# Adding the weights' lower words in one VectorE instruction, with the plan's due times set anew

## The chip, the cores and the metric

One core of a Trainium2 chip runs the program. The metric is the device time of one execution in microseconds (us), lower is better. A profiled execution gives the trace; the runs without a profile give the time.

## The reference

Random-feature attention (8 batches of 8 heads, 576 tokens, head size 64, 128 features) is followed by a two-layer network with an ELU on 4608 tokens; both weight matrices come as float64.

```python
q_s, k_s = (q * scale, k * scale)                 # q, k, v: (8, 8, 576, 64)
def phi(x):
    proj = np.einsum('bhsd,md->bhsm', x, omega)   # omega: (128, 64)
    sq = np.sum(x * x, axis=-1, keepdims=True) / 2.0
    h = proj - sq
    h = h - np.max(h, axis=-1, keepdims=True)
    return np.exp(h) / np.sqrt(m)
q_p, k_p = (phi(q_s), phi(k_s))
kv = np.einsum('bhsm,bhsd->bhmd', k_p, v)
z = np.sum(k_p, axis=2)
num = np.einsum('bhsm,bhmd->bhsd', q_p, kv)
den = np.einsum('bhsm,bhm->bhs', q_p, z)[..., None] + 1e-06
x = (num / den) laid out as (4608, 512)
h = x @ w_in                                      # (512, 2048)
g = np.where(h > 0.0, h, np.exp(np.minimum(h, 0.0)) - 1.0)
out = g @ w_out                                   # (2048, 512)
```

## The kernel before

**The work.** Two heads make a pair, and 32 pairs make the attention, four to a batch. Of a pair, keys and queries are projected (TensorE into `ppk` and `ppq`), their exponentials taken on ScalarE (`hk`, `hq`, line 463), the key-value product made (`pkv`), the queries divided by their sums on VectorE and GpSimd, turned over and multiplied by the key-value product (`pn`); ScalarE and VectorE write the result to `xh` (a rounded high part) and `xl` (the rest, line 851). The network runs in 192 steps, numbered F: a step takes 128 of the 2048 hidden units for a block of 384 tokens. Layer 1 is 12 matmuls into `ph` (lines 970 to 972, three for each of four chunks, because weights and activations are each split in a high and a low part). `ph` has two buffers, and a buffer is free once VectorE's line 983 has read it. The ELU takes two ScalarE instructions (979, 980) and that VectorE one into `e`; `e` is split into the two halves of `g` (the low half by `TENSOR_TENSOR` at the helper line 386, on GpSimd or VectorE). Layer 2 is 9 matmuls (1008 to 1010) of `g` with `w2h` and `w2l` into `acc`. Steps 0 to 23 use half the hidden units for each of blocks 0 to 2, steps 24 to 47 the other half; from step 48 on a block takes 16 steps.

**The conversion.** The weights arrive as 64-bit numbers, and `from_f64` makes 32-bit ones of them, 32 tiles of 128x512 in all (16 of the first layer, 16 of the second), most of them while blocks 0 to 2 run their first half. `raw` holds the two words of each number side by side; `u` is the tile that becomes the weight. A conversion is, in order: a load into `raw`; a scaled copy of the upper words into `u` on ScalarE (line 898); a scaled copy of the lower words in place on ScalarE (902), which leaves their top three bits as a small integer; a clamp (906), a shift (910) and the sign (915) on VectorE; the add of the lower words' bits to `u` on GpSimd (918); the high half by a copy on ScalarE or VectorE (381 or 383) and the low half by a subtraction (386) into `w1c`, or `w2h` and `w2l`.

**What sets the order.** The kernel records every piece of work as a task with an engine, a cost in ns, a due time in us and what it reads and writes. A planner (`Plan.order`) then goes through time: whenever an engine is free, it gives it the ready task with the earliest due time, by its costs and by its latencies between engines. What comes out is a fixed order for each engine; the instructions are issued in it and wait for each other by semaphores. Some tasks name a second engine and go to where the planner has them end sooner. A task with `port=True` is kept apart in time from GpSimd's tasks when it runs on VectorE. While the planned time is under `YIELD` (220 us), GpSimd's first instruction of a task is also made to wait for the VectorE task that the plan started last before it:

```python
                if eng == "POOL" or eng == "DVE" and port:
                    held[eng] = now + ns
                    if now < YIELD:
                        self.behind[best] = last.get("DVE") if eng == "POOL" else None
                    last[eng] = best
```

The due times come from the constants at the top (`MLP0`, `SEG`, `STEP`, `STEP_ATT` for the steps; `DUE_*`, `LOAD2`, `K2`, `KV2`, `Q2` for a pair's parts ahead of its end; `CONV*` for the conversions).

Of the kernel before, what the change touches and what calls it, by code (L numbers as in the profile page):

```python
# [42 lines left out]

MLP0 = 45.16
SEG = [8.6, 5.97, 3.67, 5.16, 3.34, 5.69]
STEP = 5.29
STEP_ATT = 6.32

LAG = 3.35


PAIR0 = 8.61
DUE_LOAD, DUE_K, DUE_KV, DUE_Q = 24.84, 25.17, 14.25, 18.96
LOAD2, K2, KV2, Q2 = 72.76, 36.27, 29.03, 29.75
TAIL = 12.89
TAIL2 = 5.01


CONV1 = 11.46
CONV_STEP = 0.11  # L60
CONV2 = 0.74

EARLY = 23.11
CONV3 = 52.47

# [3 lines left out]

DUE_Z = 13.38  # L70


TURNED = 8
EARLIER = 11.0
QB = 32
# [220 lines left out]

YIELD = 220e3
ENGINES = dict(DVE=mybir.EngineType.DVE, POOL=mybir.EngineType.Pool)
# [5 lines left out]
def other(kind, *engs):  # L304
    return () if ALT[kind] is None else [(eng, ns, ALT[kind]) for eng, ns in zip(engs[::2], engs[1::2])]


def mm(n, m=1):

    return m * (n / 2.23 + 2.5)  # L310


def act(n, psum=False, ptr=False):
    return (51 if psum else 93) + 0.833 * n + (93 if ptr else 0)

# [10 lines left out]
def performer_elu_kernel(  # L326
# [125 lines left out]
    def project(i, nm, due):  # L452
# [15 lines left out]
        if native(i, nm):  # L468
            for a in range(2):
                def square(e, a=a):  # L470
                    if e == "ACT":
                        nc.scalar.activation(x()[D:P, a], x()[0:D, a], AF.Square)
                    else:
                        tt(e, x()[D:P, a], x()[0:D, a], x()[0:D, a], ALU.mult)

                op(
                    "ACT", act(S), due - 3 + a, square, ((x, a),), ((x, a, 2),),
                    alt=other("sq", "POOL", pool(S), "DVE", dve(S)), port=True,
                )
            for g in range(3):  # L480
# [16 lines left out]

                op("PE", 872 if g < 2 else 240, d, mms, [*((x, a, 2) for a in range(2)), "of"], (p,))
                op(
# [20 lines left out]
        for a in range(2):  # L520
# [3 lines left out]
            op(  # L524
                "ACT", 694, due - 5 + a, lambda e, r=r, cs=cs: copy(e, y()[r, cs], x()[r, 0]), parts, ((y, a, "h"),),
                alt=other("y_hi", "DVE", dve(S, True)), port=True,
# [6 lines left out]
        for c in range(5):  # L533
# [13 lines left out]

            op("PE", mm(256, n), d, mms, [(y, a, z) for a in range(2) for z in "hl"] + ["oh", "om"], (p,))
            def rest(c=c, n=n, p2=p2, view=view):
# [145 lines left out]
    def finish(i, due):  # L695
# [25 lines left out]
        for g in range(3):  # L721
# [18 lines left out]

            op("DVE", len(slots) * 209, d, dens, (hg, pz), ((den, g),))
            op("DVE", 100, d + 0.5, lambda dg=dg: nc.vector.reciprocal(dg(), dg()), ((den, g),), ((den, g),))  # L742
# [58 lines left out]
    def output(i, halves, more=None):  # L801
# [8 lines left out]
        def mms():  # L810
# [57 lines left out]
    def from_f64(src, hi, lo, nm, due, key):  # L868
# [13 lines left out]
        def low():  # L882
            return words()[:, :, 0]
# [4 lines left out]
        def ui():  # L888
            return u().bitcast(I32)


        op(
# [267 lines left out]
```

## Time and profile before

| | |
|---|---|
| median of 3 runs | 1020.78 us (1020.41 to 1021.74) |
| the profiled execution | 1021.72 us, of which the trace's span is 1019.9 us |
| TensorE (PE) busy | 1005.0 us, 99% |
| ScalarE (ACT) busy | 698.5 us, 68% |
| VectorE (DVE) busy | 646.0 us, 63% |
| GpSimd (POOL) busy | 404.3 us, 40% |
| granted clock of TensorE | 1.0 of full speed throughout |

The span runs from the first instruction of the program to the end of the last; 1.8 us of the profiled execution lie around it. A busy share is an average over the whole span: the four engines are loaded very differently in its first 185 us, where the weights are converted, and after it.

### The profile page before, as it was taken

What the parts mean: (1) busy time and instruction counts of PE and PEld (TensorE: products, weight loads), DVE (VectorE), ACT (ScalarE), POOL (GpSimd) and SP (SyncE); (2) the same over time, 40 slices, a digit from 0 to 9 for tenths busy, and PEclk for the clock granted to TensorE, in tenths of its full rate; (3) what the DMA queues carried; (4) which work ended last, traced back from release to release, by engine and by line L of the source; (5) the groups of instructions that cost most, each with busy time, mean ns of one, the idle gap of its engine ahead of it and who ended that gap; (6) DMA issues with size and microseconds to landing.
All of it is one profiled execution on the core that took longest, in us unless ns stands there. A gap on an engine that the chain in (4) does not pass through costs nothing.

```text
span 1019.9 us, 19153 instructions
## 1 busy us (share of the span) xinstructions
PE 1005.0 (99%) x5923; PEld 890.8 (87%) x5923; DVE 646.0 (63%) x2451; ACT 698.5 (68%) x1887; POOL 404.3 (40%) x421
## 2 busy tenths in 40 slices
PE   8999999999999999999999999999999999999998
PEld 7778788998888888998888988999888888899997
DVE  6999878768978872246877874227777775222221
ACT  7989775669978983268888995338889886322222
POOL 2544444414644452233454543224445454222221
PEclk9999999999999999999999999999999999999999
DMA  8656686667697765436766867434667754533431
GB/s 212 210 194 211 217 292 229 248 201 255 224 307 237 251 212 183 158 131 219 239 209 215 246 217 243 156 124 174 229 217 229 251 155 163 186 130 132 162 128 52
DMA packets 70518, 205.24 MB, mean 201 GB/s; under 512 B 7952, under 2 KB 20432, under 8 KB 70416
## 3 DMA queue, kind: packets, MB, share of 16 engines
q1 hardware_dynamic: 70416, 204.01, 60.7%
q8 instruction: 48, 0.79, 0.3%
q14 instruction: 54, 0.44, 0.1%
HBM read 169.64 MB, written 34.34 MB: 200 GB/s over the span
## 4 chain that ended last, share of the span: by engine, by line
PE 88%; DVE 5%; ACT 4%; issue 1%; POOL 1%; DMA 1%; SPq 0%; POOLq 0%; DVEq 0%; ACTq 0%
PE ph L970 13%; PE acc L1008 12%; PE acc L1009 12%; PE ph L972 12%; PE ph L971 12%; PE acc L1010 12%; PE ppq L543 3%; PE ppk L543 3%; PE pn L820 2%; PE pkv L649 1%; PE pn L649 1%; ACT hk L463 1%; PE pkv L602 1%; PE ppq L493 1%; PE ppk L493 1%
## 5 line engine op out<-in xcount | busy, mean ns | idle before, releaser
L386 POOL TENSOR_TENSOR g<-e,g 128x384 fp32r<-128x384 f32 x173 | 183.8, 1064 | 386.9 <-DVE g L383 326.0
L970 PE MATMUL ph<-xh,w1c 128*128 128x384 f32 x768 | 263.1, 343 | 3.4 <-DVE e L983 2.7
L972 PE MATMUL ph<-xh,w1c 128*128 128x384 f32 x768 | 258.9, 337 | 0.0
L971 PE MATMUL ph<-xl,w1c 128*128 128x384 f32 x768 | 258.0, 336 | 0.0
L983 DVE SCALAR_TENSOR_TENSOR e<-e,ph 128x384 f32<-128x384 f32 x192 | 105.7, 552 | 216.7 <-ACT e L980 214.9
L979 ACT ACTIVATE e<-ph 128x384 f32<-128x384 f32 x192 | 94.8, 494 | 200.6 <-PE ph L972 193.6
L1008 PE MATMUL acc<-w2h,g 128*128 128x512 f32 x576 | 228.3, 396 | 0.0
L1009 PE MATMUL acc<-w2l,g 128*128 128x512 f32 x576 | 226.8, 394 | 0.0
L1010 PE MATMUL acc<-w2h,g 128*128 128x512 f32 x576 | 225.3, 391 | 0.0
L970 PEld LDWEIGHTS ph<-xh,w1c 128*128 128x128 f32 x768 | 144.2, 188 | 19.4 <-DVE e L983 4.8
L971 PEld LDWEIGHTS ph<-xl,w1c 128*128 128x128 f32 x768 | 144.4, 188 | 9.3
L972 PEld LDWEIGHTS ph<-xh,w1c 128*128 128x128 f32 x768 | 144.0, 187 | 0.3 <-DVE w1c L386 0.3
L1010 PEld LDWEIGHTS acc<-w2h,g 128*128 128x128 f32 x576 | 108.1, 188 | 24.6 <-POOL g L386 0.3
L1008 PEld LDWEIGHTS acc<-w2h,g 128*128 128x128 f32 x576 | 108.2, 188 | 11.4 <-issue 1.2
L1009 PEld LDWEIGHTS acc<-w2l,g 128*128 128x128 f32 x576 | 108.3, 188 | 7.9
L386 POOL TENSOR_TENSOR hq<-hq,den 128x512 f32<-128x512 f32 (+1 forms) x96 | 79.4, 839 | 76.9 <-DVE den L742 39.7
L980 ACT ACTIVATE e<-e 128x384 f32<-128x384 f32 x192 | 100.8, 527 | 3.2
L552 ACT ACTIVATE p2k<-ppk,sqk 128x128 f32<-128x128 f32 x225 | 69.7, 366 | 22.0 <-PE ppk L543 21.4
L733 DVE CUSTOM_DVE_ANT_0 junk<-hq,pz 128x128 f32<-128x128 f32 (+1 forms) x320 | 74.0, 280 | 4.6 <-PE pz L712 3.5
L561 DVE CUSTOM_DVE_ANT_0 hk<-ppk,p2k 128x128 f32<-128x128 f32 x225 | 56.9, 287 | 23.0 <-ACT p2k L552 21.9
L463 ACT ACTIVATE hk<-hk,mnk 128x128 f32<-128x128 f32 x225 | 71.2, 397 | 0.3
L463 ACT ACTIVATE hq<-hq,mnq 128x128 f32<-128x128 f32 x216 | 68.8, 404 | 0.3
(105 smaller groups left out, 1486.2 us busy)
## 6 DMA issues: line engine op xcount, KB each, us to landing
w1c<-w1s SPq DMA_DIRECT2D x176, 512.0 KB, 3.5
raw_w<-in_w_dram SPq DMA_DIRECT2D x32, 512.0 KB, 4.5
xk<-in_kx_dram SPq DMA_DIRECT2D x25, 576.0 KB, 5.0
xq<-in_qx_dram SPq DMA_DIRECT2D x24, 576.0 KB, 4.7
turned<-tb SPq DMA_DIRECT2D x24, 576.0 KB, 4.0
qh<-turned SPq DMA_DIRECT2D x96, 144.0 KB, 4.3
v<-in_v_dram SPq DMA_DIRECT2D x32, 325.0 KB, 4.2
out_dram<-o SPq DMA_DIRECT2D x36, 256.0 KB, 3.3
```

The lines of the kernel that those rows point to most:

```text
L386: (nc.vector if e == "DVE" else nc.gpsimd).tensor_tensor(*args)
L463: nc.scalar.activation(h()[:, j, :], src(j), AF.Exp, bias=mn()[:, j:j + 1], scale=-1.0)
L733: nc.vector.tensor_tensor_reduce(out=junk()[r], in0=h()[r, j, :], in1=pz()[r, a * P:(a + 1) * P], scale=1.0, scalar=EPS, op0=ALU.mult, op1 ...
L970: nc.tensor.matmul(ph(), wh, xh[:, c, o:o + TB], start=(c == 0), stop=False)
L971: nc.tensor.matmul(ph(), wh, xl[:, c, o:o + TB], start=False, stop=False)
L972: nc.tensor.matmul(ph(), wl, xh[:, c, o:o + TB], start=False, stop=(c == NC - 1))
L979: op("ACT", act(TB, True), due, lambda: nc.scalar.activation(e(), ph(), AF.Relu, scale=-1.0), (p,), (e,))
L980: op("ACT", act(TB), due + 0.2, lambda: nc.scalar.activation(e(), e(), AF.Exp, scale=-1.0), (e,), (e,))
L983: lambda: nc.vector.scalar_tensor_tensor(e(), e(), -1.0, ph(), ALU.add, ALU.max), (p, e), (e,),
L1008: nc.tensor.matmul(a(), g()[:, 0, ts], w2h[:, f], start=(f == f0), stop=False)
L1009: nc.tensor.matmul(a(), g()[:, 0, ts], w2l[:, f], start=False, stop=False)
L1010: nc.tensor.matmul(a(), g()[:, 1, ts], w2h[:, f], start=False, stop=(f == f1 - 1))
```

## The change

A conversion loses line 902 (ScalarE) and line 918 (GpSimd) and gains one VectorE instruction, which reads the lower words as unsigned integers, scales them by 2 to the minus 29 and adds them to the lower 16-bit half of each element of `u`, written as 16-bit integers at every second place. It is recorded without `port=True`. It stands at line 920 of the changed kernel; lines from 898 on move by up to four, lines 44 to 893 by one. `YIELD` goes from 220 us to 2000 us of planned time, that is, past the end. The due-time constants get new values, and a few planner costs do (a matmul of n columns, the squares, the exact size of some groups).

```diff
-MLP0 = 45.16
-SEG = [8.6, 5.97, 3.67, 5.16, 3.34, 5.69]
-STEP = 5.29
-STEP_ATT = 6.32
-LAG = 3.35
+MLP0 = 43.97
+SEG = [8.6, 6.03, 4.14, 5.3, 3.34, 5.14]
+STEP = 6.13
+STEP_ATT = 4.52
+LAG = 3.23
...
-LOAD2, K2, KV2, Q2 = 72.76, 36.27, 29.03, 29.75
+LOAD2, K2, KV2, Q2 = 88.52, 33.83, 40.2, 25.68
...
-YIELD = 220e3
+YIELD = 2e6
...
 def mm(n, m=1):
-    return m * (n / 2.23 + 2.5)
+    return m * (n / 2.32 + 8.2)
...
+        def tail():
+            return u().bitcast(U16).rearrange("p (n w) -> p n w", w=2)[:, :, 0]
...
         op(
-            "ACT", 571, due - 6.5,
-            lambda: nc.scalar.activation(low(), low().bitcast(U32), AF.Copy, scale=2.0 ** -29), ((raw, 0),), ((raw, 0),),
-        )
...
-        op("POOL", 1274, due - 5, lambda: nc.gpsimd.tensor_tensor(ui(), ui(), low(), ALU.add), (u, (raw, 0)), (u,))
+        op(
+            "DVE", dve(512), due - 5,
+            lambda: nc.vector.scalar_tensor_tensor(tail(), low().bitcast(U32), 2.0 ** -29, tail(), ALU.mult, ALU.add),
+            (u, (raw, 0)), (u,),
+        )
```

The order of all engines changes. The first place is VectorE's row ahead of the ELU of steps 16 and 17 of the network, in the middle of the second layer's conversions (`u_w2_12` is tile 12 of the second layer on its way, `e_16` the ELU of step 16). Before:

```order
L983 SCALAR_TENSOR_TENSOR e_15_1984<-e_15_1984,ph_15_1946 128x384
L915 SCALAR_TENSOR_TENSOR u_w2_13_1970<-raw_w2_13_1923,u_w2_13_1970 128x512
L386 TENSOR_TENSOR g_15_2006<-e_15_1984,g_15_2006 128x384
L906 TENSOR_SCALAR u_w2_14_2016<-u_w2_14_2016 128x512
L383 CAST w2h_80<-u_w2_12_1935 128x512
L910 TENSOR_SCALAR u_w2_14_2016<-u_w2_14_2016 128x512
L386 TENSOR_TENSOR w2l_81<-u_w2_12_1935,w2h_80 128x512
L915 SCALAR_TENSOR_TENSOR u_w2_14_2016<-raw_w2_14_1972,u_w2_14_2016 128x512
L983 SCALAR_TENSOR_TENSOR e_16_2031<-e_16_2031,ph_16_1988 128x384
L983 SCALAR_TENSOR_TENSOR e_17_2049<-e_17_2049,ph_17_2019 128x384
```

The same place of the changed kernel, where line 920 is the new instruction, 384 and 387 are the helper lines 383 and 386, and 987 is line 983:

```order
L987 SCALAR_TENSOR_TENSOR e_15_1955<-e_15_1955,ph_15_1930 128x384
L920 SCALAR_TENSOR_TENSOR u_w2_10_1944<-raw_w2_10_1903,u_w2_10_1944 128x512
L384 CAST w2h_80<-u_w2_10_1944 128x512
L387 TENSOR_TENSOR w2l_81<-u_w2_10_1944,w2h_80 128x512
L987 SCALAR_TENSOR_TENSOR e_16_1994<-e_16_1994,ph_16_1970 128x384
L384 CAST g_16_2012<-e_16_1994 128x384
L906 TENSOR_SCALAR u_w2_11_2010<-u_w2_11_2010 128x512
L910 TENSOR_SCALAR u_w2_11_2010<-u_w2_11_2010 128x512
L915 SCALAR_TENSOR_TENSOR u_w2_11_2010<-raw_w2_11_1961,u_w2_11_2010 128x512
L920 SCALAR_TENSOR_TENSOR u_w2_11_2010<-raw_w2_11_1961,u_w2_11_2010 128x512
L987 SCALAR_TENSOR_TENSOR e_17_2031<-e_17_2031,ph_17_2006 128x384
```

The pieces of three conversions stood among each other: a conversion's high half (`w2h` of tile 12) came after the first piece of tile 14, since GpSimd's add lay ahead of it, and `e_16` and `e_17` behind all of them. Now a conversion's add, high and low half follow each other, `e_16` comes right behind the low half of tile 10, and `e_17` behind four pieces of tile 11.

The second place is GpSimd's row at the same steps (`g_13` is the low half of step 13). Before:

```order
L386 TENSOR_TENSOR g_13_1925<-e_13_1902,g_13_1925 128x384
L918 TENSOR_TENSOR u_w2_11_1879<-u_w2_11_1879,raw_w2_11_1824 128x512
L386 TENSOR_TENSOR g_14_1960<-e_14_1943,g_14_1960 128x384
L918 TENSOR_TENSOR u_w2_12_1935<-u_w2_12_1935,raw_w2_12_1874 128x512
L918 TENSOR_TENSOR u_w2_13_1970<-u_w2_13_1970,raw_w2_13_1923 128x512
L918 TENSOR_TENSOR u_w2_14_2016<-u_w2_14_2016,raw_w2_14_1972 128x512
L918 TENSOR_TENSOR u_w2_15_2073<-u_w2_15_2073,raw_w2_15_2023 128x512
L386 TENSOR_TENSOR g_18_2136<-e_18_2094,g_18_2136 128x384
```

And of the changed kernel:

```order
L387 TENSOR_TENSOR g_13_1897<-e_13_1879,g_13_1897 128x384
L387 TENSOR_TENSOR g_14_1938<-e_14_1918,g_14_1938 128x384
L387 TENSOR_TENSOR g_15_1975<-e_15_1955,g_15_1975 128x384
L387 TENSOR_TENSOR g_16_2012<-e_16_1994,g_16_2012 128x384
L387 TENSOR_TENSOR g_17_2057<-e_17_2031,g_17_2057 128x384
L387 TENSOR_TENSOR g_18_2113<-e_18_2073,g_18_2113 128x384
L387 TENSOR_TENSOR g_19_2187<-e_19_2097,g_19_2187 128x384
```

Five of eight rows were adds of the conversion, and steps 15 to 17 had their low half made on VectorE; now the row holds one low half after the other, those of steps 15 to 17 too.

## Rows read from the trace of the kernel before

**Rows 1.** The page's first part: busy time of each engine in us, its share of the span, and its instructions.
```profile
span 1019.9 us, 19153 instructions
PE 1005.0 (99%) x5923; PEld 890.8 (87%) x5923; DVE 646.0 (63%) x2451; ACT 698.5 (68%) x1887; POOL 404.3 (40%) x421
```

**Rows 2.** Busy time of each engine in four stretches of the span; the first runs from the first matmul of step 0 of the MLP (44.1) to that of step 8 (116), the second from there to that of step 24 (185). Columns: the stretch, its length, then busy us (and instructions) of PE, of its weight loads, of VectorE (DVE), ScalarE (ACT) and GpSimd (POOL), then the granted clock, the DMA share and GB/s.
```profile
44.10:116.00 71.90, 66.16 (x442) 54.17 (x440) 68.96 (x244) 65.44 (x170) 35.96 (x34) 1.00 0.59 198
116.00:185.00 69.00, 67.06 (x343) 59.26 (x344) 53.56 (x110) 42.99 (x92) 28.49 (x24) 1.00 0.72 260
200.00:400.00 200.00, 199.64 (x1215) 176.33 (x1215) 148.39 (x617) 161.30 (x458) 85.96 (x93) 1.00 0.72 237
800.00:1000.00 200.00, 200.00 (x1098) 180.47 (x1097) 77.20 (x286) 89.51 (x231) 65.06 (x69) 1.00 0.48 159
```

**Rows 3.** What TensorE (PE) waited for: line, the releaser, then us in total, times, longest. The first eight rows are all but one (0.2 us) of the stretch from 20 to 180 us; the last row is the only one from 180 us to the end.
```profile
PE ph L970 <- DVE e L983: 2.7, 4, 1.3
PE pkv L597 <- ACT hq L463: 1.2, 2, 0.7
PE ppq L493 <- DVE xl L851: 1.1, 1, 1.1
PE ppq L493 <- DVE w2l L386: 0.8, 1, 0.8
PE ph L970 <- DVE den L733: 0.5, 1, 0.5
PE pn L815 <- ACT hq L463: 0.3, 1, 0.3
PE pn L815 <- ACT hk L463: 0.3, 1, 0.3
PE pkv L597 <- DVE xl L851: 0.3, 1, 0.3
PE ppk L543 <- ACT kvf L381: 0.4, 1, 0.4
```

**Rows 4.** The timeline around 159 us, engine by engine (GpSimd, VectorE, TensorE): start, us, engine, line, operation, out<-in, and in brackets the idle time before it and what ended it.
```profile
157.50 1.38 POOL L918 TENSOR_TENSOR u_w<-u_w,raw_w 128x512 int32<-128x512 int32 x1 [1.15 <-issue]
157.29 0.42 DVE L906 TENSOR_SCALAR u_w<-u_w 128x512 f32<-128x512 f32 x1
158.91 0.43 DVE L383 CAST w2h<-u_w 128x512 fp32r<-128x512 f32 x1 [1.21 <-POOL u_w L918]
159.59 0.68 DVE L386 TENSOR_TENSOR w2l<-u_w,w2h 128x512 fp32r<-128x512 f32 x1
160.20 0.68 DVE L915 SCALAR_TENSOR_TENSOR u_w<-raw_w,u_w 128x512 int32<-128x512 int32 x1
160.80 1.01 DVE L983 SCALAR_TENSOR_TENSOR e<-e,ph 128x384 f32<-128x384 f32 x2
...
161.40 0.45 PE L970 MATMUL ph<-xh,w1c 128*128 128x384 f32 x1 [1.30 <-DVE e L983]
```

**Rows 5.** The timeline around 55 us (GpSimd, VectorE, TensorE), same columns.
```profile
54.69 1.29 POOL L918 TENSOR_TENSOR u_w<-u_w,raw_w 128x512 int32<-128x512 int32 x1 [1.02 <-DVE w2h L383]
55.23 1.30 DVE L386 TENSOR_TENSOR w2l<-u_w,w2h 128x512 fp32r<-128x512 f32 x1
...
56.54 0.44 PE L493 MATMUL ppq<-of,xq 128*64 128x128 f32 x4 [0.84 <-DVE w2l L386]
57.27 0.49 PE L597 MATMUL pkv<-v,hk 128*128 128x130 f32 x2 [0.28 <-DVE xl L851]
```

**Rows 6.** The timeline around 50 us (ScalarE, then VectorE), same columns.
```profile
49.48 0.69 ACT L902 ACTIVATE raw_w<-raw_w 128x512 int32<-128x512 uint32 x1
50.06 0.69 ACT L381 CAST xh<-pn 128x256 fp32r<-128x256 f32 x2
50.45 0.82 DVE L851 TENSOR_TENSOR xl<-pn,xh 128x256 fp32r<-128x256 f32 x2
```

**Rows 7.** Three lines of the conversion: the operation and its count, then duration in ns (least/median/longest), first and last start in us, shape.
```profile
L902 ACT ACTIVATE raw_w<-raw_w x32: 657/678/807, 23.4 to 202.9; 128x512 int32<-128x512 uint32 x32
L918 POOL TENSOR_TENSOR u_w<-u_w,raw_w x32: 1289/1308/1769, 31.7 to 210.0; 128x512 int32<-128x512 int32 x32
L915 DVE SCALAR_TENSOR_TENSOR u_w<-raw_w,u_w x32: 673/684/1705, 30.0 to 208.6; 128x512 int32<-128x512 int32 x32
```

**Rows 8.** VectorE's waits for the removed GpSimd instruction: us in total, times, longest.
```profile
DVE w2h L383 <- POOL u_w L918: 5.4, 5, 1.2
DVE w1c L383 <- POOL u_w L918: 2.2, 3, 1.5
```

**Rows 9.** The first and the last of six VectorE instructions between 44 and 116 us that ran long beside the removed GpSimd instruction (for the last one, GpSimd's row stands ahead of it). Columns as in group 4.
```profile
53.12 1.10 DVE L915 SCALAR_TENSOR_TENSOR u_w<-raw_w,u_w 128x512 int32<-128x512 int32 x1
...
105.59 1.31 POOL L918 TENSOR_TENSOR u_w<-u_w,raw_w 128x512 int32<-128x512 int32 x1
106.14 1.31 DVE L915 SCALAR_TENSOR_TENSOR u_w<-raw_w,u_w 128x512 int32<-128x512 int32 x1
```

**Rows 10.** Pair 16 of the attention, TensorE and ScalarE: the last projection of its keys, the last five exponentials of them, and the key-value product that reads them. Columns as in group 4; the last row's 18 matmuls are merged.
```profile
448.47 0.28 PE L543 MATMUL ppk<-om,tk 128*128 128x256 f32 x1
...
451.74 1.57 ACT L463 ACTIVATE hk<-hk,mnk 128x128 f32<-128x128 f32 x5
...
459.98 1.20 PE L649 MATMUL pkv<-hk,v 128*64 128x128 f32 x18
```

More of the change, by code (lines that the diff above doesn't have):

```diff
@@ L12 @@
 I32 = mybir.dt.int32
+U16 = mybir.dt.uint16
 U32 = mybir.dt.uint32
@@ L41 @@
 NNAT = dict(k=7, q=8)
-MLP0 = 45.16
-SEG = [8.6, 5.97, 3.67, 5.16, 3.34, 5.69]
-STEP = 5.29
-STEP_ATT = 6.32
-LAG = 3.35
-PAIR0 = 8.61
-DUE_LOAD, DUE_K, DUE_KV, DUE_Q = 24.84, 25.17, 14.25, 18.96
-LOAD2, K2, KV2, Q2 = 72.76, 36.27, 29.03, 29.75
[L55 to L64, printed above, removed]
+MLP0 = 43.97
[3 more added lines that the diff above has]
+LAG = 3.23
+PAIR0 = 7.98
+DUE_LOAD, DUE_K, DUE_KV, DUE_Q = 24.72, 24.58, 15.2, 19.06
+LOAD2, K2, KV2, Q2 = 88.52, 33.83, 40.2, 25.68
+TAIL = 9.89
+TAIL2 = 5.24
+CONV1 = 10.73
+CONV_STEP = -0.42
+CONV2 = 1.65
+EARLY = 24.36
+CONV3 = 44.25
 SPLIT = (0, 8, 16)
 NHALF = 3
-DUE_Z = 13.38
+DUE_Z = 11.27
 TURNED = 8
-EARLIER = 11.0
+EARLIER = 11.17
 QB = 32
@@ L476, in project @@
                 op(
-                    "ACT", act(S), due - 3 + a, square, ((x, a),), ((x, a, 2),),
-                    alt=other("sq", "POOL", pool(S), "DVE", dve(S)), port=True,
+                    "ACT", 690, due - 3 + a, square, ((x, a),), ((x, a, 2),),
+                    alt=other("sq", "POOL", 1190, "DVE", 750), port=True,
                 )
@@ L496, in view @@
                     return p().rearrange("p (j x) -> p j x", j=4)
-                op("PE", 872 if g < 2 else 240, d, mms, [*((x, a, 2) for a in range(2)), "of"], (p,))
+                op("PE", 872 if g < 2 else 340, d, mms, [*((x, a, 2) for a in range(2)), "of"], (p,))
                 op(
@@ L524, in project @@
             op(
-                "ACT", 694, due - 5 + a, lambda e, r=r, cs=cs: copy(e, y()[r, cs], x()[r, 0]), parts, ((y, a, "h"),),
+                "ACT", 565, due - 5 + a, lambda e, r=r, cs=cs: copy(e, y()[r, cs], x()[r, 0]), parts, ((y, a, "h"),),
                 alt=other("y_hi", "DVE", dve(S, True)), port=True,
@@ L546, in view @@
                 return p().rearrange("p (a x) -> p a x", a=2)
-            op("PE", mm(256, n), d, mms, [(y, a, z) for a in range(2) for z in "hl"] + ["oh", "om"], (p,))
+            op("PE", mm(256, n) + 20, d, mms, [(y, a, z) for a in range(2) for z in "hl"] + ["oh", "om"], (p,))
             def rest(c=c, n=n, p2=p2, view=view):
@@ L739, in dg @@
                 return den()[:, js]
-            op("DVE", len(slots) * 209, d, dens, (hg, pz), ((den, g),))
+            op("DVE", len(slots) * 209 + (180 if g == 2 else 0), d, dens, (hg, pz), ((den, g),))
             op("DVE", 100, d + 0.5, lambda dg=dg: nc.vector.reciprocal(dg(), dg()), ((den, g),), ((den, g),))
@@ L831, in output @@
         op(
-            "PE", 4 * mm(S) + 200 + ns, d, mms, [*((qh, g) for g in parts), ("kvf", i % 2), *reads],
+            "PE", 4 * mm(S) + 100 + ns, d, mms, [*((qh, g) for g in parts), ("kvf", i % 2), *reads],
             [p for _, _, p in halves],
@@ L898, in from_f64 @@
             lambda: nc.scalar.activation(u(), up().bitcast(F32), AF.Copy, scale=2.0 ** -112), ((raw, 1),), (u,),
-        )
-        op(
-            "ACT", 571, due - 6.5,
-            lambda: nc.scalar.activation(low(), low().bitcast(U32), AF.Copy, scale=2.0 ** -29), ((raw, 0),), ((raw, 0),),
         )
```

## The prediction

> **What bounds the kernel now.** I read the page's engine shares first, because they say which engine can set the time at all. TensorE is busy for 1005.0 of 1019.9 us [rows 1]; only some 15 us of the span are left to win without taking matmuls away, and the change takes none away. Then I asked for busy time by stretch, because a share of 99% can hide one bad stage. From 200 us on TensorE is full (199.64 and 200.00 of 200 us), while VectorE, ScalarE and GpSimd have room. Between 44.1 and 116 us three engines are near their limit at once: TensorE 66.16, VectorE 68.96 and ScalarE 65.44 of 71.9 us. From 116 to 185 us VectorE falls to 53.56 of 69 us [rows 2]. All conversions but the last few lie in these two stretches. Third, TensorE's own waits: the eight rows from 20 to 180 us sum to 7.2 us, and all name VectorE or ScalarE; after 180 us there is one wait of 0.4 us. No row names GpSimd [rows 3]. So the reader should see a kernel that is a full TensorE with 7.2 us of holes in its first 180 us, and every term below is a hole that closes or opens. How busy the other engines are counts only where it makes one.
>
> **What makes the holes.** I followed the largest ones back. At 161.40 us TensorE had stood still for 1.30 us, since both `ph` buffers waited for line 983. That stood on VectorE behind the high and low half of one conversion and the sign of another, and the high half had itself waited 1.21 us for GpSimd's add of line 918, which ran from 157.50 to 158.88 [rows 4]. A single instruction that waits for GpSimd thus held everything queued behind it, the ELU too. At 55.23 us a low half took 1.30 us, where another took 0.68 [rows 4, 5]; it began while line 918 was running (54.69 plus 1.29), and TensorE waited 0.84 us for it and 0.28 us for the `xl` queued next [rows 5]. At 49.48 us line 902 took ScalarE for 0.69 us just ahead of the copy to `xh`, which `xl` follows and which the wait of 1.1 us is about [rows 3, 6].
>
> **What goes.**
> Line 918, 32 times 1308 ns on GpSimd [rows 7], was not on TensorE's path by its own length. It is worth what it did to VectorE. The holes of 1.30, 0.84 and 0.28 us sum to 2.4, and I count them as closed: **-2.4 us**. The new order supports this at the first of them: ahead of `e_16` no sign of a later tile stands any more, and three instructions follow `e_15` where there were seven. The bounds are 0 (something else is late at the same place) and -3.9, if all 2.7 us of line 983's waits go with the other two.
> Line 902, 32 times 678 ns on ScalarE [rows 7], was ahead of `xh` once: **-0.7 us** of the hole of 1.1. The holes that name `hq` and `hk` (1.2, 0.3 and 0.3) are exponentials that come late on a crowded ScalarE. There 13 of the removed instructions stood between steps 0 and 8 in the order, 13 x 0.68 = 8.8 us of 65.44 [rows 2, 7]. Two copies of high halves move to ScalarE in the new order by step 8. Its idle time in that stretch still about doubles from 6.5 us, and I take three quarters of the 1.8 us: **-1.3 us** (bounds 0 and -1.8).
>
> **What comes.** The trace has no instruction that writes 16-bit halves at every second place. The nearest row is line 915: the same engine and form, 512 elements, one operand from `raw` at every second word, median 684 ns [rows 7]. I take 0.684. Below it 0.5 could be argued from line 983 (1.01 us for two, overlapped, of 384 elements [rows 4]); above it 1.37, twice line 915, if half-word writes run at half rate.
> Between steps 0 and 8 the order has 13 of them: 13 x 0.684 = 8.9 us more for an engine with 71.9 - 68.96 = 2.9 us idle [rows 2]. Against that, one copy (0.43) and two low halves (0.68 each [rows 4]) leave VectorE, 1.8 us. And instructions no longer run long beside line 918: six did in this stretch, the first by 1.10 - 0.68 = 0.42 us and the last by 0.63 [rows 7, 9], the one at 55.23 us by 0.62; at about 0.6 each that is 3.7 us. The net is 8.9 - 1.8 - 3.7 = 3.4 us, 0.5 us more than the idle time. Between steps 8 and 24 there are 11 more, 7.5 us against 15.4 us idle, and 7.6 us of VectorE's waits for line 918, over the whole run, go [rows 2, 8]; five low halves of `g` move to GpSimd besides. They fit, though on a fuller engine the ELU comes later now and then. For both stretches I count **+1.0 us** (bounds 0 and +9, the latter at 1.37 us each: 13 x 0.69 on top).
>
> One rule speaks against this. Line 915 took up to 1705 ns against 673 [rows 7], and the long ones of group 9 lie beside a GpSimd instruction. The Trainium skill, page SBUF — State Buffer, section "SBUF: two separate sides", says that VectorE instructions with two SBUF inputs and GpSimd's instructions share one port pair as an exclusive lock, and whoever starts second is blocked. The trace agrees with it. By that rule the new instruction, which reads `raw` and `u` and is recorded without `port=True`, queues behind whatever GpSimd runs. Without the rule, from rows: GpSimd keeps 35.96 - 13 x 1.31 = 18.9 of 71.9 us there [rows 2, 7], so about one in four meets it and waits about half of such an instruction, 0.5 us: 13 x 0.26 x 0.5 = 1.7 us. That is on the slow rival's side.
>
> **What moves.** The due times only set the order. From 185 us on the order could only lose, since TensorE is full there. The tightest new place that I found is the key-value product of the pairs: pair 16 had 60 matmuls between its last `ppk` and `pkv`, now 31; ten pairs have 21 to 31 where they had 48 to 63. A matmul costs on average 200 / 1098 = 0.182 us [rows 2], so 3.8 to 5.6 us now lie between. The exponentials need 453.31 - 448.47 = 4.8 us from that `ppk`, with 6.7 us to spare before [rows 10]. Five pairs could wait, up to 1 us each, so 0 to +3; the exponentials move with the due times too, and I take **+0.8 us**. GpSimd's waits in plan order after 220 us cost nothing, as TensorE waits for GpSimd nowhere [rows 3] and GpSimd is under half busy [rows 2]; if that cover went, a low half of `g` would be late by one VectorE instruction, some 0.7 us. The last matmuls and copies stand as before.
>
> **Sum.** -2.4 - 0.7 - 1.3 + 1.0 + 0.8 = -2.6 us. It is made on the profiled execution (1021.72 us, 1.8 around the span); that lies 0.9 us over the median of 1020.78, and the shift is carried to the median: **1018.2 us**.
>
> **Rivals.**
> *Nothing is won* (0.25): the holes name line 983, `xl` and `hq`, which stay, and VectorE stays 96% full between steps 0 and 8. If what closes at three places opens at others, 4.4 us are given back: 1020.3 us. Against it: the pieces that held the queue are gone by name.
> *Slower* (0.18): the new instruction is longer than its model, in VectorE's fullest stretch. With a price p the overflow there is 13p - 1.8 - 3.7 - 2.9 us, and the time is past +2 us when that reaches 5.6, so from p = 1.08 us. At 1.2 us it overflows by 7.2: 1020.78 - 4.4 + 7.2 + 0.8 = 1024.4 us. For it speaks the lock above and a form with no row; against it that a typical instruction of the length took 0.684.
> *All holes close* (0.12): the new order also removes the rest of the 7.2 us, 1013.6 us. For it: conversions no longer block one another; against it: no order made VectorE or ScalarE idle there before.
> The forecast keeps 0.45.
>
> **How the numbers follow.** About 0.2% (2 us) is what a measurement of this kernel can tell from no change. The forecast's own range is 1016.3 to 1019.6, and a quarter of its chance falls within 0.2%; so faster is 0.34 + 0.12 and 0.03 of the even case, 0.49; same is 0.11 + 0.21 of the even case, 0.32; slower is the slow case and 0.01 of the even one, 0.19. The range starts at the case without holes, 1013.6, and reaches to 1022.8, which leaves out most of the slow case.
>
> **What the profile would show.** Right: the new instruction near 0.68 us, no wait of VectorE for GpSimd in the conversions, fewer `hq` rows among TensorE's waits, the sum of its waits from 20 to 180 us at 4 to 5 us, and next to none after. Wrong on the slow side: the new instruction over 1 us, or line 983 naming more than 2.7 us. Wrong in another place: waits for `hk` at `pkv` after 200 us, or a low half of `g` that TensorE waits for.

## The result, and the profile after

The changed kernel takes **1026.8 us** (median; 1024.5 to 1032.3), the kernel before 1020.8 in the same session: a ratio of 1.0060, interval 1.0045 to 1.0075, so some 6 us slower. Predicted was 1018.2, in a range of 1013.6 to 1022.8. The profiled execution took 1025.25 us, with this first part of the page (to be read against [rows 1]):

```profile
span 1023.5 us, 19117 instructions
PE 1010.0 (99%) x5923; PEld 890.8 (87%) x5923; DVE 646.6 (63%) x2465; ACT 681.0 (67%) x1865; POOL 363.6 (36%) x397
```

TensorE issues the same 5923 matmuls and is busy for 5.0 us more; 1.7 us of this is one stretch at a lower granted clock, which only some executions have (last section). Its waits from 20 to 180 us, and then from 180 us to the end (columns as in [rows 3]):

```profile
PE ppq L494 <- ACT qh L382: 1.6, 1, 1.6
PE ph L974 <- DVE e L987: 0.9, 1, 0.9
PE pt L757 <- ACT qh L382: 0.8, 1, 0.8
PE ppq L494 <- ACT hk L464: 0.6, 1, 0.6
PE pt L757 <- POOL hq L387: 0.6, 1, 0.6
PE ph L974 <- ACT kvf L382: 0.4, 1, 0.4
...
PE ph L974 <- DVE e L987: 0.7, 1, 0.7
PE ph L974 <- DMA w1c<-w1s: 0.4, 1, 0.4
PE acc L1012 <- DVE o L1026: 0.2, 1, 0.2
PE ppk L544 <- DVE mnq L562: 0.2, 1, 0.2
```

The first six sum to 4.9 us against 7.2, and the last four to 1.5 against 0.4. The waits fell by about 1 us in all, yet the kernel is slower. So the loss is not in what TensorE waits for but in how long it works. The new instruction (line 920) and the stretches of [rows 2] read:

```profile
L920 DVE SCALAR_TENSOR_TENSOR u_w<-raw_w,u_w x32: 728/754/1553, 30.8 to 215.1; 128x512 uint16<-128x512 uint32 x32
...
44.10:116.00 71.90, 67.42 (x447) 57.80 (x447) 70.73 (x234) 58.79 (x158) 26.10 (x25) 0.98 0.59 197
116.00:185.00 69.00, 69.00 (x367) 61.07 (x365) 55.75 (x115) 38.86 (x83) 17.74 (x17) 1.00 0.73 257
800.00:1000.00 200.00, 200.00 (x1070) 178.66 (x1069) 70.14 (x252) 81.16 (x201) 58.65 (x62) 1.00 0.45 152
```

The place to look is the end of the program, where the two kernels do the same thing: the second layer of the last steps, with the same copy on VectorE and the same subtraction on GpSimd beside it, before and after (timeline of TensorE: start, length, line):

```profile
1010.04 0.39 PE L1008 MATMUL acc<-w2h,g 128*128 128x512 f32 x1
1010.27 0.39 PE L1009 MATMUL acc<-w2l,g 128*128 128x512 f32 x1
1010.50 0.39 PE L1010 MATMUL acc<-w2h,g 128*128 128x512 f32 x1
1010.72 0.39 PE L1008 MATMUL acc<-w2h,g 128*128 128x512 f32 x1
...
1012.78 0.39 PE L1008 MATMUL acc<-w2h,g 128*128 128x512 f32 x1
```

```profile
1014.15 0.40 PE L1012 MATMUL acc<-w2h,g 128*128 128x512 f32 x1
1014.39 0.39 PE L1013 MATMUL acc<-w2l,g 128*128 128x512 f32 x1
1014.62 0.40 PE L1014 MATMUL acc<-w2h,g 128*128 128x512 f32 x1
1014.86 0.39 PE L1012 MATMUL acc<-w2h,g 128*128 128x512 f32 x1
...
1016.95 0.40 PE L1012 MATMUL acc<-w2h,g 128*128 128x512 f32 x1
```

Twelve matmuls take 2.74 us before (228 ns each) and 2.80 after (233). That holds all through: the mean from the start of one `acc` matmul to that of the next, over the 1300 or so that follow each other directly, is 230.0 ns before and 233.1 after. I call this the pace. It leaves out some 25 pairs that start over 0.3 us apart; with them it is 231.9 and 234.8, and these are the figures in the expectations of e1 to e3. For `ph`, counted in the same way, the pace is 175.0 and 174.7. The kernel has 1728 `acc` matmuls, and 1728 x 3.1 = 5.4 us is the size of what is missing. The programs differ in one thing that these matmuls could notice. A buffer pool gives out addresses in the order of first use, and the new order uses the small `sqk` buffers after `e` and `g`: the first `g` buffer lies at byte 215232 of each partition, before at 215360.

### The profile page after: what moved, and what is told of

Read it like the earlier page. It is cut to its first block, busy times and chain, and to the rows that moved or that the text cites. A ratio compares the mean times of both kernels' runs of the same rounds, so it can differ in the third digit from the quotient of the medians.

```text
span 1023.5 us, 19117 instructions
## 1 busy us (share of the span) xinstructions
PE 1010.0 (99%) x5923; PEld 890.8 (87%) x5923; DVE 646.6 (63%) x2465; ACT 681.0 (67%) x1865; POOL 363.6 (36%) x397
## 4 chain that ended last, share of the span: by engine, by line
PE 77%; ACT 2%; DMA 1%; DVE 1%; issue 0%; ACTq 0%
PE acc L1012 11%; PE acc L1013 11%; PE ph L974 11%; PE acc L1014 11%; PE ph L976 11%; PE ph L975 11%; PE ppq L544 2%; PE ppk L544 2%; PE pn L821 2%; PE pkv L650 1%; PE pn L650 1%; PE pz L713 1%; DMA raw_w<-in_w_dram 1%; ACT hq L464 0%; ACT p2q L553 0%
## 5 line engine op out<-in xcount | busy, mean ns | idle before, releaser
L387 POOL TENSOR_TENSOR g<-e,g 128x384 fp32r<-128x384 f32 x176 | 181.7, 1032 | 482.6 <-DVE g L384 343.4
L987 DVE SCALAR_TENSOR_TENSOR e<-e,ph 128x384 f32<-128x384 f32 x192 | 105.7, 551 | 232.5 <-ACT e L984 226.0
L553 ACT ACTIVATE p2k<-ppk,sqk 128x128 f32<-128x128 f32 x225 | 67.4, 366 | 4.3 <-DVE den L734 2.0
L562 DVE CUSTOM_DVE_ANT_0 hq<-ppq,p2q 128x128 f32<-128x128 f32 x216 | 53.9, 285 | 25.8 <-ACT p2q L553 24.6
```

What stands on the lines that cost most here:

```text
L387: (nc.vector if e == "DVE" else nc.gpsimd).tensor_tensor(*args)
L562: nc.vector.tensor_tensor_reduce(out=h()[:, j, :], in0=view()[:, a, 0:M], in1=p2()[:, a, :], scale=1.0, scalar=HIGHEST, op0=ALU.add, op1=A ...
L987: lambda: nc.vector.scalar_tensor_tensor(e(), e(), -1.0, ph(), ALU.add, ALU.max), (p, e), (e,),
```

## Experiments

Times are medians; the kernel before stood at 1021.3 to 1021.6 in the sessions with several runs. Ratios are to it, with 95% intervals, over the runs of both; they need not be the quotient of the medians (for e5 that is 1.0004, and the ratio 1.0015).

**The place of `g`, from both sides.** e1 puts an unused tile into the changed kernel; e2 claims `e` and `g` first in the kernel before.

```diff
+PADS = {"e": 32}
 ...
             pool, shape, dtype, name = self.args
+            n = PADS.pop(self.key, 0)
+            if n:
+                pool.tile([128, n], F32, tag="pad", bufs=1, name="pad")
```

> The changed kernel with one edit: an unused tile of 128 bytes ahead of the two e buffers, so that e, g and what lies above them stand at the SBUF addresses of the kernel before (first g buffer at byte 215360 of each partition, in the changed kernel 215232; the order in which buffers are first used moved it). Order of instructions, waits and tables stay those of the changed kernel. Theory A (the acc matmuls, whose weights are the g tiles, run at a pace that goes with where g lies: start to start 231.9 ns before, 234.8 after, also in the last 36 acc matmuls where nothing else changes): acc back at 229 to 231 ns, and 1726 x 3 ns = 5 us less than the changed kernel, 1020 to 1022.5 us; by TensorE's waits, which fell by some 2 us, it may come out under the kernel before. Theory B (GpSimd's waits in plan order, or more traffic beside TensorE, slow it): as the changed kernel, 1025 to 1029. Theory C (the new tables give TensorE a worse order of pieces): 1025 to 1029. Theory D (each loading of a program has a pace of its own by chance): a spread as wide as that of the changed kernel, 1024 to 1032.

```diff
             pool, shape, dtype, name = self.args
+            if self.key == "sqk" and FIRST:
+                FIRST.clear()
+                pool.tile([128, TB], F32, tag="e", bufs=2, name="e_first")
+                pool.tile([128, 2, TB], F32R, tag="g", bufs=3, name="g_first")
```

> The kernel before with one edit: the e and g buffers are claimed before the small sqk buffers, so that e and g stand 128 bytes lower, where the changed kernel has them (first g at byte 215232), and sqk 12 KB higher. Nothing else changes. Theory A: acc matmuls at 233 to 235 ns start to start instead of 231.9, 1727 x 3 ns = 5 us slower than the kernel before: 1024 to 1027 us. Theories B and C: as the kernel before, 1020 to 1022. Theory D: by chance either.

e1: 1023.75 us, 1.0022 (1.0011 to 1.0034), `acc` pace 230.0 ns. e2: 1025.66 us, 1.0046 (1.0031 to 1.0060), pace 232.7. Theory A holds both ways: the kernel before gets slower by moving `g` alone, and the changed kernel gets its pace back. But e1 stays 2.2 us over the kernel before, where the waits were to put it under. Its waits from 20 us on sum to 9.3 us, against 6.4 in the changed kernel and 7.8 in the kernel before: part of what the quicker matmuls save seems to come back as waiting.

**GpSimd's waits; the tail alone.** e3 sets `YIELD` back in the changed kernel. e4 takes only the part of the diff in `from_f64` into the kernel before (lines 902 and 918 out, the tail in).

```diff
-YIELD = 2e6
+YIELD = 220e3
```

> The changed kernel with YIELD back at 220e3: GpSimd waits for VectorE in plan order only up to 220 us of the plan. Buffers stay where the changed kernel has them. Theory A: no change that the runs can tell, 1025 to 1029, acc at 234 to 235 ns. Theory B: 1020 to 1023, acc at 231 to 232. Theory C: as the changed kernel, 1025 to 1029.

> The kernel before with the tail alone: VectorE's instruction on 16-bit halves in place of ScalarE's and GpSimd's, due times, costs and YIELD as before. In this kernel too the first use of buffers puts g at byte 215232. Theory A: the loss of 5 us by g's place, less up to 2.6 us that the tail takes out of TensorE's waits by the prediction: 1023 to 1027, acc at 233 to 235 ns. Theories B and C (the loss is in YIELD or in the tables): 1018 to 1022 with acc at 231 to 232.

e3: 1027.96 us, 1.0073 (1.0057 to 1.0089), pace 233.1. e4: 1027.65 us, 1.0061 (1.0039 to 1.0082), pace 232.6. Theories B and C fall as causes of the pace. e4 loses as much as the whole change: the tail changes the order of first use too. (Of its four runs the one with a mean granted clock of 1.0 took 1024.28 us; the others, at 0.996 to 0.999, took 1027.5 to 1028.9.)

**The tail with `g` back (e5), `w1c` moved too (e6).** e4 with `PADS = {"e": 32}`, and with `PADS = {"w1c": 32}`.

> The kernel before with the tail alone (as e4) and 128 unused bytes ahead of the e buffers, so that e and g stand where the kernel before has them (g at byte 215360). Theory A (g's place sets the pace of the acc matmuls): acc at 229 to 231 ns as in the kernel before and in e1, and 4.6 to 5.2 us under e4 (1027.65), 1022 to 1023.5. What is left against the kernel before is then the tail alone: theory A1 (the tail closes holes of TensorE, as predicted: idle 9.0 us in e4's profile against 10.2 before) 1019 to 1021; theory A2 (what VectorE is given costs more than it closes, as e4 standing 2 us over e2 hints) 1022 to 1024.

> As e5, but the 128 unused bytes lie ahead of the w1c buffers: g again at byte 215360, and w1c, which the ph matmuls have as their weights, at 200000 in place of 199872. The remainder of an address by 512 was 320 for g where acc was quick and 192 where it was slow; w1c had 192 in every kernel so far and has 320 here. Theory A3 (what counts is where the weights of a matmul lie in 512 bytes, whichever matmul): ph, at 174 to 176 ns start to start in every kernel so far, becomes quicker by 1 to 4 ns, 2304 of them 2 to 9 us: 1012 to 1020. Theory A4 (g's place counts in some other way, by e and g against each other or against DMA writes): ph as before, the time as e5's.

e5: 1021.67 us, 1.0015 (1.0006 to 1.0025), paces 230.2 and 175.1. A1 falls: with `g` in place, the tail still wins nothing. e6: 1020.40 us, 0.9990 (0.9981 to 0.9999), `ph` pace 173.5. The place of `w1c` counts for `ph` as that of `g` does for `acc`.

**Three places in one kernel.** e4 with longer `g` buffers, so that each has its own remainder; e8 has `PADS = {"g": 48}` as well.

```diff
-        g = gt[F] = Buf(sb, [P, 2, TB], F32R, "g", f"g_{F}", 3)
+        g = gt[F] = Wide(sb, [P, 2 * TB + 16], F32R, "g", f"g_{F}", 3)
```

> As e4 (tail alone), with each g buffer 64 bytes longer, so that its three buffers lie at 215232, 218368 and 221504: remainders 192, 256 and 320 by 512; e stays where e4 has it. Theory A with g alone: acc at 232 to 234 ns on the first buffer (192) and 229 to 231 on the third (320), the second unknown. If it is e's place that counts, all three stand at 232 to 234.

> As e7 with 192 unused bytes ahead of g: its buffers at 215424, 218560 and 221696, remainders 384, 448 and 0 by 512. Theory A: some of these may be quicker or slower than 229; if the pace goes with the place inside 256 bytes, 448 is as 192 (232 to 234) and 64 as 320; no pace was measured yet for 384 and 0.

Pace of `acc` by `g` buffer in e7, worked out from the starts in the trace:

```
g at 215232 (remainder 192): 232.5 ns, 449 matmuls
g at 218368 (remainder 256): 231.9 ns, 436
g at 221504 (remainder 320): 230.1 ns, 436
```

One program, one execution, every `acc` matmul at the full granted clock, and the pace goes with the buffer; `e` had not moved. In e8 it is 231.2 (384), 232.9 (448) and 231.6 (0). Each ran once, for 1025.22 and 1029.76 us; e8 had the lower clock from 11.8 to 22.0 us, before its first `acc`.

**Both kernels with both places put right.** e9 is the kernel before with `PADS = {"w1c": 32, "g": 96}`; e10 the changed kernel with `PADS = {"w1c": 32}`.

> The kernel before, nothing changed but two unused tiles: 128 bytes ahead of w1c and 384 ahead of g, so that the weights of ph (w1c, first buffer at byte 200000) and of acc (g, 215872) both lie at remainder 320 by 512. Theory A3 (the place of a matmul's weights sets its pace): ph at 173.4 ns start to start as in e6 in place of 174.9, 2304 x 1.5 = 3.5 us, acc as before: 1017 to 1018.5. If e6's gain came from something else that the tail brought, 1021 as the kernel before.

> The changed kernel with 128 unused bytes ahead of w1c: w1c and g both at remainder 320. Theory A3: 3.5 us under e1 (1023.75), 1019.5 to 1021.5, and 2 to 3 us above e9, which is what tail, tables and GpSimd's waits do together once the places are the same. By the steps of the prediction, which put these at -2.6, it would stand at 2 to 3 us under e9, 1014.5 to 1016.

e9: **1018.50 us**, 0.9975 (0.9966 to 0.9984), paces 230.1 and 173.5: two unused tiles make it faster than both kernels. e10: 1022.72 us, 1.0017 (1.0004 to 1.0031), same paces. With the places equal the change costs 1.0017 - 0.9975 = 0.42%, 4.3 us, where the prediction's steps gave -2.6. (e1 and the kernel before have equal places too, and differ by 2.2; the intervals of the two figures overlap.)

**The removal alone (e11), the tail twice (e12).** e11 leaves the lower words out; e12 is e5 with a second instruction like the tail and the factor 0.0.

> The kernel before without the two instructions that add the lower words (ScalarE's L902 and GpSimd's L918) and without the tail: the lower words of the weights are left out. g falls at 215360, w1c at 199872, as in the kernel before. It measures the removal alone. Prediction's steps (holes made by L918 close, 2.4, and that of L902, 0.7): 3.1 under the kernel before, 1017.5 to 1018.5. Rival (the holes move to the next late instruction of VectorE, which stays 96% busy from 44 to 116 us): 1020 to 1021.3. Against e5 (1021.67, the same with the tail) the difference is the tail's own cost: 1.0 by the prediction, 3 or more if it eats the whole gain.

> e5 (tail alone, g at 215360) with a second tail for each of the 32 tiles, multiplied by 0.0, so that it adds nothing: it doubles VectorE's added work, 32 x 0.7 us, of which some 20 in the stretches that are full. Prediction's price for a tail's 0.68 us in a full stretch: 1.0 for 24 of them, so 1022.5 to 1023. Rival (each tail stands in VectorE's queue ahead of the mn and xl instructions that release TensorE's banks, as at 55.8 us in e5): 3 to 6 more than e5, 1024.5 to 1027.5.

e11: 1019.25 us, 0.9980 (0.9971 to 0.9989): the removal gives 2.0 us, where 2.4 + 0.7 + 1.3 = 4.4 were predicted (the expectation of e11 leaves out the 1.3, which the prediction counted for line 902 in the new order). Against it e5 shows the tail's price: 0.35%, 3.6 us (2 to 5 by the two intervals), where 1.0 was predicted. e12: 1036.85 us, 1.0162: another 32 tails cost 15 us more, far over the rival's 3 to 6.

The clock has a share in all three. In e11 the granted clock falls at 60.4 us, after a wait of 1.95 us (0.61 from 60 to 62 us, 0.54 from 62 to 64), which costs 2 x 0.39 + 2 x 0.46 = 1.7 us, and all eleven of its runs show a mean clock of 0.996 to 0.998. Of e5's twelve, five show 0.997 or 0.998 and took 1024.1 us on average, the other seven 1021.4. So without the clock the removal would give some 3.7 us, an estimate from these figures, and the tail would still take all of it back. In e12 the mean clock is 0.991 to 0.993, so up to some 8 of its 15 us are time at the lower clock.

In e5 the place of the hole of [rows 5] reads (VectorE, ScalarE, TensorE):

```profile
53.19 0.73 DVE L926 SCALAR_TENSOR_TENSOR u_w<-raw_w,u_w 128x512 uint16<-128x512 uint32 x1
53.82 0.68 DVE L508 TENSOR_REDUCE mnq<-ppq 128x4 f32<-128x512 f32 x1
54.41 0.42 DVE L390 CAST w1c<-u_w 128x512 fp32r<-128x512 f32 x1
54.74 0.68 DVE L921 SCALAR_TENSOR_TENSOR u_w<-raw_w,u_w 128x512 int32<-128x512 int32 x1
55.35 0.81 DVE L858 TENSOR_TENSOR xl<-pn,xh 128x256 fp32r<-128x256 f32 x2
...
53.73 0.37 ACT L388 CAST xh<-pn 128x256 fp32r<-128x256 f32 x1 [1.17 <-PE pn L822]
...
55.79 0.44 PE L500 MATMUL ppq<-of,xq 128*64 128x128 f32 x4 [1.57 <-DVE xl L858]
```

The first half of `xh` is ready at 54.10, but `xl` starts at 55.35. VectorE has no gap: it works off the tail, a minimum, a high half and a sign first. The hole that line 918 had made (0.84 and 0.28) is closed, and one of 1.57 us made by the queue stands there. The stretch from 44.1 to 116 us, for e11, e5 and e12 (columns as in [rows 2]):

```profile
44.10:116.00 71.90, 67.92 (x446) 56.94 (x445) 68.22 (x241) 57.52 (x154) 22.18 (x22) 0.98 0.65 213
...
44.10:116.00 71.90, 67.12 (x442) 54.81 (x441) 70.69 (x251) 56.95 (x156) 25.57 (x24) 1.00 0.62 207
...
44.10:116.00 71.90, 60.73 (x373) 50.53 (x372) 69.00 (x224) 52.02 (x136) 24.74 (x23) 0.91 0.55 185
```

VectorE, whose busy time stands fourth among the us, stays at 95% in e11 although line 918 no longer holds it up (68.22 us, before 68.96). In e5 it is at 98%, and in e12 TensorE issues 69 matmuls fewer in the stretch than in e5, at a granted clock of 0.91.

**Waits or tables.** e13 is e5 with `YIELD` at 2e6; e14 is e1 with `YIELD` at 220e3.

> e5 (tail alone, g at 215360) with YIELD at 2e6: GpSimd waits for VectorE in plan order throughout, tables as in the kernel before. Theory W (the waits cost what is left, GpSimd starting late in the attention of the later blocks): 1 to 2.5 above e5 (1021.67), 1022.7 to 1024. Theory T (the tables do): as e5, 1021 to 1022.3.

> The changed kernel with YIELD back at 220e3 and 128 unused bytes ahead of e, so g at 215360: tail and tables without the waits. Theory T (the new tables open holes of TensorE between 185 and 300 us, 3.6 us in e1's profile, 1.8 in e3's, against 0 to 0.6 with the old tables, while the 2.3 of 116 to 185 us close): as e1, 1023 to 1024.5. Theory W: as e5, 1021 to 1022.3.

e13: 1022.11 us, 1.0006 (0.9996 to 1.0016), beside e5 at 1.0015: the waits cost nothing that can be told. e14: 1024.20 us, 1.0027 (1.0017 to 1.0037), as e1. So what remains goes with the tables: 0.7 us by e1 against e5, 1.2 by e14 against e5 and 2.8 by e10 against e6, each to within some 1.5 us. Part of it shows in e1 after 180 us, where e5 has a single wait of 0.2 us:

```profile
PE ph L980 <- DMA w1c<-w1s: 0.9, 2, 0.5
PE ph L980 <- DVE e L993: 0.7, 1, 0.7
PE ppk L550 <- DVE mnq L568: 0.4, 1, 0.4
PE ppq L550 <- ACT kvf L388: 0.4, 1, 0.4
PE acc L1018 <- DVE o L1032: 0.2, 1, 0.2
```

These sum to 2.6 us. TensorE is also busy for longer from 20 us on, 990.6 us in e1 against 989.2 in e5, at the same paces; what makes it so is open.

**Place or distance.** Theory A3 says that the remainder itself counts. e15 and e17 shift operands together, in the kernel before:

```diff
+    const.tile([P, 32], F32, name="pad")
     w2h = const.tile([P, NF, DM], F32R, name="w2h")
```

> The kernel before with 128 unused bytes ahead of w2h, so that everything from w2h and xh upward (weights, their other operands, all buffers) lies 128 bytes higher: w1c at remainder 320 by 512, g at 448, and the distance of each to the other operand of its matmul as in the kernel before. If the place itself counts: ph at 173.4 ns start to start, acc at 233. If the distance counts: ph at 175, acc at 230, as in the kernel before.

e17 has the same line ahead of `xh` instead.

> The kernel before with 128 unused bytes between w2l and xh: w2h and w2l stay, xh, xl, w1c, e, g and all other buffers lie 128 bytes higher. From w2h to g the distance by 512 is then 320 in place of 192 (e8 had 320 in its second buffer, acc 232.9); from xh to w1c it stays 64. Theory A5 (the distance between a matmul's two operands sets its pace): acc at 232 to 234 ns start to start, ph at 175. If the distance of g to any other buffer counts, acc stays at 230.

All `acc` work from 880 to 1000 us, where TensorE is full, in the kernel before, e2, e15 and e17 (stretch, length, TensorE's busy us and matmuls, then its weight loads and the other engines):

```profile
880.00:1000.00 120.00, 62.38 (x252) 46.80 (x252) 0.00 (x0) 3.26 (x6) 1.00 0.41 141
...
880.00:1000.00 120.00, 63.74 (x252) 46.85 (x252) 0.00 (x0) 3.26 (x6) 1.00 0.42 139
...
880.00:1000.00 120.00, 62.54 (x252) 46.48 (x251) 0.00 (x0) 3.26 (x6) 1.00 0.42 141
...
880.00:1000.00 120.00, 63.86 (x252) 46.51 (x251) 0.00 (x0) 3.27 (x6) 1.00 0.42 141
```

The same 252 matmuls take 62.4 and 62.5 us where `g` and `w2h` keep their distance (before, e15), and 63.7 and 63.9 where it changed (e2, e17). Paces: e15 230.2 and 175.0, e17 233.1 and 174.0. A3 falls: in e15 `g` stands at 448 and is quick, `w1c` at 320 and is not. For `acc`, A5 holds: e17 left `w2h` and `w2l` in place, and the pace went with `g`'s distance to them. For `ph` it misses a little: the distance stayed 64 and the pace went from 175.0 to 174.0, so something besides it counts. From kernel to kernel the pace at one and the same distance differs by up to 0.6 ns for `acc` (at 64: 232.5 in e7, 233.1 in the changed kernel) and 1.6 for `ph` (at 64: 174.0 in e17, 175.6 in e8).

**Other distances.** e16 has three places for `w1c` (`Wide` as in e7, `PADS = {"w1c": 80}`), e18 finer ones for both.

> The kernel before with each w1c buffer 64 bytes longer and 320 unused bytes ahead of them: its three buffers at remainders 0, 64 and 128 by 512 (g at 320 as before). Places not seen yet for ph, which had 175.0 at 192 and 173.5 at 320. If 320 is the best place, these three stand at 174 to 177; if 64 is as 320 (the place inside 256 bytes counts), the second stands at 173.5.

> The kernel before with each w1c and g buffer 32 bytes longer and unused bytes ahead of both: w1c at distances 160, 192 and 224 by 512 from xh, g at 448, 480 and 0 from w2h. Theory A5: the second w1c buffer has ph at 173.4 ns as in e9; the others show whether 192 is a peak; for g no value was seen at these three (ph had 173.6 at 448 and 175.6 at 0).

With e7, e8 and e9, the pace in ns by the distance, by 512 bytes, from a matmul's other operand (`w2h`, `xh`) to its weights (`g`, `w1c`), each from one buffer of one kernel:

```
distance    0     64    128   160   192   224   256   320   384   448   480
acc       231.7  232.5 231.9        230.1       231.2 232.9 231.6 230.4 232.1
ph        175.6  175.0       176.3  173.5 174.9             177.0 173.6
```

192 and 448 are the quickest for both kinds; of the places tried none beats e9's. Distances 256 bytes apart go together wherever both were tried: for `acc` 0 and 256, 64 and 320, 128 and 384, 192 and 448 lie within 0.5 ns of each other, for `ph` 192 and 448 within 0.1. So the distance by 256 bytes would do as well. The single times of e15 to e18 (1022.2, 1022.0, 1023.2 and 1023.2 us) show little by themselves; those of e16 and e18 mix three places.

## Why the prediction was wrong

Step by step, in us, by the ratios above:

| step | predicted | measured |
|---|---|---|
| lines 918 and 902 go | -2.4 - 0.7 - 1.3 | -2.0 (e11), interval -3.0 to -1.1; some -3.7 without its fall of the clock |
| the tail comes | +1.0 | +3.6 (e5 against e11), about +2 to +5 |
| the order by the new tables | +0.8 | +0.7 (e1 against e5) to +2.8 (e10 against e6) |
| GpSimd's waits | 0 | 0 (e13), to within 1 us |
| "The last matmuls and copies stand as before" | 0 | +3.9 (the changed kernel against e1) |

- **The largest miss is the last line**, and the sentence in front of the argument that the change takes no matmuls away, so that every term is a hole. I held TensorE's 1005.0 us for fixed and listed only what it waits for. A matmul's length is not fixed here: the change moved `g` by 128 bytes, and 1728 matmuls went from 230.0 to 233.1 ns. In the new order one could read that `e` and `g` come before `sqk`; I compared what stands on each engine and not where the buffers come to lie.
- **The tail's price was mis-sized**, +1.0 for a measured +3.6. One part is its duration: the median of 754 ns is near the 684 assumed, but the 13 tails from 44 to 116 us took 11.4 us in the changed kernel and 10.1 in e5, where 8.9 were assumed. The other is the step from an overflow of 0.5 us to +1.0 us. An engine at 96% delays TensorE by each instruction that stands ahead of one that TensorE waits for, whatever its overflow; e5 shows that at 54 us, behind a tail of 0.73 us, and e12 points the same way. The slow rival also looked for the loss in VectorE's fullest stretch, but asked for a tail of more than 1.08 us, and the median came at 0.75.
- **The holes closed as predicted, and others opened.** The hole of 1.30 at 161 us [rows 4] is gone (from 116 to 185 us TensorE is busy for 69.00 of 69.00), as are VectorE's waits for line 918. Waits that name ScalarE's `hq` and `hk` fell from 1.8 to 0.6 us (in e11 to 0.7). In their place stand two for `qh`, 1.6 and 0.8, which is ScalarE's copy after a transpose: ScalarE is less busy from 44 to 116 us (58.79 us for 65.44), and yet another of its customers is late. One of 0.6 names GpSimd, which none did before. That is the rival "what closes at three places opens at others", and it held alongside the pace. Its time was added up wrongly: 4.4 us given back on 1018.2 make 1022.6, not 1020.3. So corrected it lies close to e1, the run with the old pace (2.2 us over the kernel before), though there the parts are others. (A smaller slip: the bound of -3.9 for line 918 comes to -3.8.)
- **Right**: no wait for `hk` at `pkv` appeared after 180 us, and GpSimd's waits cost nothing. Waits between 20 and 180 us came out at 4.9, inside the 4 to 5 named; "next to none after" was wrong, with 1.5 us for 0.4. "From 185 us on the order could only lose" was right too, but the waits were for the ELU and for `w1c`'s loads (e1), not at `pkv`.

The rule that I weighed, VectorE's lock with GpSimd, did touch the tail: in the changed kernel eight of 32 took 903 to 1553 ns, each while an instruction of GpSimd was running. Five of them lie between 44 and 116 us and are 1.7 us longer than at the median, just what the prediction worked out from rows and then left out of its sum. It did not decide e5's largest hole, which stands behind a tail of 0.73 us.

## What to carry over

When the engine that bounds a kernel is full, compare the pace of its instructions as well as its waits: start to start, in a stretch where nothing else differs. A change of order can move buffers, so list their addresses before and after; if a time moves with no wait to show for it, shift one buffer by 128 bytes in the old kernel. On an engine that is 96% full, price an added instruction by what is queued behind it, not by the idle time left. And before a step of one or two us is priced, compare the granted clocks of the runs: a single fall is as large.

## What the runs showed of the hardware

**A matmul's pace goes with the distance of its operands in SBUF**, the on-chip memory that both are read from: 230.1 to 232.9 ns for 512 columns and 173.5 to 177.0 for 384, both in 32-bit form, by the table above. The Trainium skill, page SBUF — State Buffer, section "Who interferes with whom", gives TensorE two read ports, independent, one for the moving operand and one for weight loads, and says that TensorE never waits on anyone. Nothing here shows a wait for another engine, but the two operands of TensorE's own matmuls are not without effect on each other; e7, and e15 beside e17, decide that. How they meet is open: no run looked inside a matmul.

**The granted clock fell after a wait of 1.57 us in some executions.** In the changed kernel (timeline around 99 us; ScalarE, then TensorE) the transposes end and `qh`'s copy stands behind other work of ScalarE:

```profile
97.41 1.28 ACT L464 ACTIVATE hk<-hk,mnk 128x128 f32<-128x128 f32 x4
98.59 0.85 ACT L553 ACTIVATE p2k<-ppk,sqk 128x128 f32<-128x128 f32 x3
99.34 0.58 ACT L382 COPY qh<-pt 128x512 f32<-128x512 f32 x1
...
99.97 0.82 PE L494 MATMUL ppq<-of,xq 128*128 128x128 f32 x5 [1.57 <-ACT qh L382]
```

Granted clock around it (the third figure from the end), first for the changed kernel, then for e1, which has the same wait at 102 us:

```profile
98.00:100.00 2.00, 0.42 (x5) 1.00 0.16 49
100.00:102.00 2.00, 2.00 (x13) 0.69 0.57 213
102.00:104.00 2.00, 2.00 (x8) 0.50 0.40 162
104.00:106.00 2.00, 2.00 (x16) 0.96 0.25 100
...
100.00:102.00 2.00, 0.44 (x4) 1.00 0.25 31
102.00:104.00 2.00, 1.73 (x13) 1.00 0.59 231
104.00:106.00 2.00, 2.00 (x12) 1.00 0.38 152
```

At 0.50, the lower of its two levels (1.2 GHz), the changed kernel loses 2 x 0.31 + 2 x 0.50 + 2 x 0.04 = 1.7 us, and e1 nothing. Ten of the traces have one wait of 1.57 or 1.58 us; in three (the changed kernel, e6, e7) the clock falls after it, in seven (e4 and e5 among them) it doesn't. After 1.95 us in e11 it falls, after 2.19 in e14 it doesn't. So such a hole can cost about twice its length. What decides it is open: a mean clock of 0.998 or less is shown by all eleven runs of e11, six of ten of e6 and three of nine of e14. In the kernel before, whose trace has no wait over 1.30 us after 20 us, 13 of the 82 runs beside the experiments still show 0.998; these took 1022.5 us on average, the others 1021.1. This widens the spread, but it doesn't account for the one run at 1032 us, which stays open.

**The start differs between executions of one plan.** TensorE from 4 to 8 us, before and after:

```profile
4.00:8.00 4.00, 3.04 (x15) 1.00 1.03 260
...
4.00:8.00 4.00, 3.11 (x24) 1.00 1.01 251
```

24 matmuls against 15 in the same time: those of 128 columns follow each other at 112 ns from 5.7 us on in one and, at 213 ns until then, from 10.3 us in the other. e1 has the plan of the changed kernel and starts like the kernel before (112 ns from 9.8 us). The rows give a granted clock of 1.00 for both, but the traces' clock records begin only at 5.2 us in the changed kernel, 10.2 in the kernel before and 9.2 in e1. So the clock ahead of that is not shown; a rise from the lower level to the higher at these times would fit. The profiled execution of the changed kernel had the early start, by which it was 21 matmuls ahead at 20 us (127 for 106, 2.3 us at 112 ns). That is one reason why the gap of the two profiles (3.5 us) is smaller than that of the medians (6.0).
